# Hash attention and an MLP on one core: the scale row and its product moved to the front, hash products ahead of the fillers, the last unit's sums cut in halves

## The chip, the cores and the metric

The kernel runs on one core of a Trainium2 chip. A core has TensorE (PE; its weight loads are listed as PEld), VectorE (DVE), ScalarE (ACT), GpSimd (POOL) and SyncE (SP), which here only issues DMAs. Each engine executes its own instructions in the order in which they were written and waits on semaphores for the others. Matrix products land in PSUM, everything else lies in SBUF, inputs and outputs in the chip's memory (HBM). The metric is the device time of one execution in microseconds (us); the median of several runs is given. The profile is one further execution, recorded by the hardware profiler.

## The reference

Two layers. First, attention with a hash mask: q and k get six sign bits each from a random projection, and a query sees only the keys with the same six bits.

```python
q_bits = (np.einsum('bhsd,dk->bhsk', q, proj) > 0)
k_bits = (np.einsum('bhsd,dk->bhsk', k, proj) > 0)
mask = q_bucket[:, :, :, None] == k_bucket[:, :, None, :]
scores = np.where(mask, scale * np.matmul(q, k.transpose(0, 1, 3, 2)), -1000000000.0)
attn = softmax(scores)                       # + 1e-09 in the denominator
x = np.matmul(attn, v)                       # -> (B, S, H * D)
xn = (x - mu) / np.sqrt(var + 1e-06) * g_ln  # over the last axis
out = x + np.maximum(xn @ w_ch1, 0.0) @ w_ch2
```

The shapes: 4 batches, 8 heads, 768 positions, 64 numbers per head; the MLP goes from 512 to 2048 and back. All inputs and the output are f32.

## The kernel before

**Units.** The work is cut in 12 units `u`: batch `u // 3`, and 256 of the 768 queries, all eight heads. Within a unit there are two groups `g` of four heads and three pieces `kp` of 256 keys; `s` from 0 to 71 counts unit, group and piece.

**The order is written out by hand.** `ORDER` is one long string of words such as `S.t.0.2`: a function's name, the engine (t TensorE, v VectorE, a ScalarE, p GpSimd, s SyncE) and its arguments. The program walks through it and issues each word's instructions to its engine. What counts on the chip is only the order of the words of one engine among themselves, and who waits for whose data or buffer. `SLOTS` gives, for each kind of tile, which of its few buffers the next new tile takes; a tile waits until the last user of the buffer's former tile is done. PSUM has three large buffers (`pp`: scores `sc`, sums `acc`, and the tile of the fillers) and two small ones (`f`: everything else).

**The words that the change and the prediction touch**, with the line of their instruction in the profile:

- `lx`, `lv` (L373, L465) load q, k and v of batch 0; `LX`, `lv` (L508, L467) those of the later batches; `lw1`, `lw2` (L446, L457, from GpSimd) the weights; `lg` (L433) the row `moe_g_ln`. `gx` (L505) is a one-column memset through which a load waits for its buffer.
- `warm` (L363) eight products of ones with ones; `wm` (L366) one more such product each. They compute nothing that is used and are called fillers.
- `tn` (L304) turns a piece of q (t = 0) or k (t = 1) of batch 0, two transposes each; `ca` (L311 to L315) casts the turned piece to bf16; `ha` (L394) is the hash product of a piece, `bh` (L307) makes its bits; `hc`, `bc`, `sl`, `bi` (L405, L307, L418, L428/L430) do the same in another layout for the later q pieces. For batches 1 to 3 it is `tu` (L304, eight pieces), `CA`, `hm` (L526) and `bt` (L307), and the bits go through HBM (`mw`, `mr`, L544 and L547).
- `S` (L570) scores of one `s`: the bits as extra rows of the product, then q by k. `E` (L576) the exponential of two heads. `A` (L595) attention weights by v, summed in `acc`. `cv` (L473, L475) casts v; `sq` (L494) or `su`/`sp` sum v over the keys, `sc` (L500, L502) copies that sum, for rows in which the mask leaves nothing.
- `na`, `nb` (L608 to L617) normalise, `nc`, `ag`, `ce`, `rs` (L621 to L636) are the layer norm.
- `gt` (L437) turns the row `moe_g_ln` into a column, with eight small products, `gc` (L443) copies it to `gT`. In unit 0 the normalised x is transposed on TensorE (`ft`, L644) and scaled with gT on the way out (`fc`, L652); later units go through a DMA transpose (`fl`, L639), and `wg` (L452, L454) scales the weights with gT once.
- `F` (L659) an eighth of the first MLP product, `R` (L667, L669) its relu. In unit 0 the second product is plain (`D`, `Z`). From unit 1 on it is done by seven products of half-size blocks instead of eight: `P` (L725) the products 1 to 7, `ss` (L710) the four sums of blocks of the hidden layer that they need, `sw` (L699) those of the weights, once, and `Y` (L730) adds products to the output. `O` (L742, L744) stores.

The sums that `ss` makes, for `k` = 1 to 4, each over eight blocks of 128 hidden numbers by 128 queries:

```python
1: (1, Hq(u, 1, 0), Hq(u, 1, 1), AOP.add),
2: (2, None, Hq(u, 0, 0), AOP.subtract),          # None: sum 1
3: (3, Hq(u, 0, 0), Hq(u, 1, 0), AOP.subtract),
4: (4, Hq(u, 0, 1), None, AOP.subtract),          # None: sum 2
```

Block `n` of the halves comes from products `F` 0, 1 (blocks 0 to 3), 2, 3 (4 to 7), 4, 5 (8 to 11) and 6, 7 (12 to 15).

## Time and profile before

| what | us |
|---|---|
| median of three runs | 295.71 (293.08 to 297.33) |
| the profiled execution | 294.86 |
| its span in the trace | 293.2 |
| TensorE busy | 285.6 (97% of the span) |
| VectorE busy | 206.8 (71%) |
| ScalarE busy | 206.2 (70%) |
| GpSimd busy | 54.0 (18%) |

A row of the instructions in order of time reads: start, duration, engine, line, operation, what it writes and reads, the shapes, how many, and in brackets the idle time of the engine ahead of it and who ended that. A row with several instructions runs from the start of the first to the end of the last. A matmul's recorded duration is longer than its step, since products overlap in the array; the distance of starts is the step. A row of the busy time by stage gives the stretch, its length, and the busy time (and count) of TensorE, weight loads, VectorE, ScalarE and GpSimd in it, then the clock granted to TensorE, the share of the DMA engines and GB/s. The chain of work that ended last is followed back from the last instruction.

### The profile page before, as it was taken

What the parts mean: (1) busy time and instruction counts of PE and PEld (TensorE: products, weight loads), DVE (VectorE), ACT (ScalarE), POOL (GpSimd) and SP (SyncE); (2) the same over time, 40 slices, a digit from 0 to 9 for tenths busy, and PEclk for the clock granted to TensorE, in tenths of its full rate; (3) what the DMA queues carried; (4) which work ended last, traced back from release to release, by engine and by line L of the source; (5) the groups of instructions that cost most, each with busy time, mean ns of one, the idle gap of its engine ahead of it and who ended that gap; (6) DMA issues with size and microseconds to landing.
All of it is one profiled execution on the core that took longest, in us unless ns stands there. A gap on an engine that the chain in (4) does not pass through costs nothing.

```text
span 293.2 us, 10524 instructions
## 1 busy us (share of the span) xinstructions
PE 285.6 (97%) x4650; PEld 227.7 (78%) x4650; DVE 206.8 (71%) x474; ACT 206.2 (70%) x236; POOL 54.0 (18%) x88
## 2 busy tenths in 40 slices
PE   8999999999999999999999999999999999999994
PEld 4677778648788887878778778877888878897883
DVE  4757899996769795797667995866666654773433
ACT  4689999998966978784865896887793694515240
POOL 5261325222423005000300107210010010000000
PEclk9999999999999999999999999999999999999999
DMA  6999997747744692362330352230410402304022
GB/s 223 302 319 250 216 277 133 139 134 171 174 122 131 134 307 76 127 189 51 98 82 1 83 132 63 60 61 3 92 37 2 74 2 52 78 6 104 2 72 73
DMA packets 31055, 34.10 MB, mean 116 GB/s; under 512 B 15521, under 2 KB 27809, under 8 KB 31010
## 3 DMA queue, kind: packets, MB, share of 16 engines
q1 hardware_dynamic: 25938, 28.72, 35.6%
q0 software_dynamic: 4224, 4.19, 8.9%
q8 instruction: 36, 0.59, 0.9%
q10 hardware_dynamic: 848, 0.53, 0.7%
q14 instruction: 9, 0.07, 0.1%
HBM read 27.86 MB, written 6.88 MB: 118 GB/s over the span
## 4 chain that ended last, share of the span: by engine, by line
PE 91%; DMA 3%; DVE 2%; SPq 1%; ACT 1%; issue 0%; ACTq 0%; DVEq 0%
PE f L659 27%; PE sc L570 18%; PE X L725 13%; PE acc L595 12%; PE Yb L725 7%; PE hp L526 3%; PE Ya L725 3%; PE hf L394 3%; PE f L674 2%; PE warm L363 1%; ACT E L576 1%; DMA G<-Bd 1%; DMA Bd<-B 1%; PE warm L366 1%; DMA xnT<-xc 1%; SPq L547 1%
## 5 line engine op out<-in xcount | busy, mean ns | idle before, releaser
L576 ACT ACTIVATE E<-sc,bias_sb 128x1024 bf16<-128x1024 f32 x144 | 153.1, 1111 | 36.0 <-PE sc L570 32.6
L659 PE MATMUL f<-xnT,w_sb 128*128 128x256 bf16 x768 | 94.2, 273 | 0.7 <-DMA xnT<-xc 0.6
L659 PEld LDWEIGHTS <-w_sb 128*128 128x128 bf16 x768 | 71.4, 98 | 13.6 <-issue 5.7
L667 ACT ACTIVATE hb<-f 128x512 bf16<-128x512 f32 x67 | 39.6, 598 | 34.5 <-PE f L659 34.5
L570 PE MATMUL sc<-qb,kb 32*128 32x256 bf16 x1152 | 52.5, 267 | 0.0
L595 PEld LDWEIGHTS <-E 128*128 128x128 bf16 x1152 | 40.8, 98 | 4.0 <-issue 2.5
L595 PE MATMUL acc<-vaug,E 128*128 128x65 bf16 x1152 | 43.7, 194 | 0.1
L570 PE MATMUL sc<-G 6*128 6x256 bf16 (+1 forms) x576 | 42.7, 273 | 1.1 <-ACT E L576 0.8
L725 PEld LDWEIGHTS <-hb 128*128 128x128 bf16 x352 | 33.4, 98 | 5.4 <-issue 1.3
L570 PEld LDWEIGHTS <-kb 32*128 32x128 bf16 x1152 | 30.5, 93 | 1.5
L635 POOL TENSOR_SCALAR rs<-mv 128x2 f32<-128x2 f32 x12 | 3.3, 277 | 150.4 <-DVE mv L624 150.4
L730 DVE TENSOR_TENSOR x<-X,x 128x256 f32<-128x256 f32 x44 | 18.4, 419 | 16.5 <-PE X L725 16.3
L570 PEld LDWEIGHTS <-G 6*128 6x128 bf16 (+1 forms) x576 | 16.0, 91 | 16.7 <-issue 13.3
L725 PEld LDWEIGHTS <-S 128*128 128x128 bf16 x264 | 25.0, 98 | 4.8 <-issue 1.4
L669 DVE TENSOR_SCALAR hb<-f 128x512 bf16<-128x512 f32 x29 | 19.7, 681 | 12.0 <-PE f L659 11.8
L304 DVE STREAM_TRANSPOSE T<-X 128x384 f32<-128x384 f32 (+2 forms) x52 | 26.1, 535 | 0.0
L725 PE MATMUL Yb<-w_sb,S 128*128 128x256 bf16 x176 | 22.9, 273 | 0.0
L608 DVE SCALAR_TENSOR_TENSOR y<-vsB,acc 128x520 f32<-128x520 f32 x24 | 16.5, 689 | 8.1 <-PE acc L595 7.8
L725 PE MATMUL X<-wt,hb 128*128 128x256 bf16 x168 | 21.8, 273 | 0.0
L617 DVE TENSOR_TENSOR x<-y,rc 128x512 f32<-128x512 f32 x24 | 17.8, 742 | 0.8
L621 DVE BATCH_NORM_STATS2 st<-x 128x6 f32<-128x256 f32 x48 | 17.4, 412 | 0.2
L730 DVE TENSOR_TENSOR x<-Yb,x 128x256 f32<-128x256 f32 x22 | 9.2, 420 | 9.5 <-PE Yb L725 9.5
(95 smaller groups left out, 268.3 us busy)
## 6 DMA issues: line engine op xcount, KB each, us to landing
out_dram<-x SPq DMA_DIRECT2D x45, 128.0 KB
X<-in_k_dram SPq DMA_DIRECT2D x7, 768.0 KB
vn<-in_v_dram SPq DMA_DIRECT2D x24, 192.0 KB
X<-in_q_dram SPq DMA_DIRECT2D x6, 768.0 KB
w_sb<-in_moe_w_ch_dram POOLq DMA_DIRECT2D x8, 512.0 KB, 10.8
vn<-in_v_dram SPq DMA_DIRECT2D x2, 768.0 KB
X<-in_q_dram SPq DMA_DIRECT2D x2, 512.0 KB
Bd<-B SPq DMA_DIRECT2D x6, 96.0 KB
```

What stands on the lines that cost most here:

```text
L304: nc.vector.transpose(d[:, j], s[:, j, kj0 : kj0 + n])
L570: nc.tensor.matmul(sc(s, i // 2)[:, i % 2, 256 * kk : 256 * kk + 256], lh, rh, start=(rep == 0), stop=(rep == 2), skip_group_check=True,)
L576: nc.scalar.activation(E(s)[:, heads(h)], sc(s, h), AF.Exp, scale=EXP_SCALE, bias=bias_sb)
L595: nc.tensor.matmul(acc[:, qt, (D + 1) * i : (D + 1) * (i + 1)], E(s)[:, i, 256 * kk + P * qt : 256 * kk + P * qt + P], vaug(u // 3)[:, 4 * ...
L608: nc.vector.scalar_tensor_tensor(yt(u, g), vs, EPS_ROW, made[f"acc{u}{g}"][:, :, :A], op0=AOP.mult, op1=AOP.add,)
L617: nc.vector.tensor_tensor(xo, a[:, :, :, 0:D], rc.to_broadcast([P, 2, 4, D]), op=AOP.mult)
L621: nc.vector.bn_stats(stats(u)[:, qt, g], xt(u)[:, qt, 256 * g : 256 * g + 256])
L659: nc.tensor.matmul(f1[:, n].rearrange("p (t x) -> p t x", t=2), w1_sb[:, dt, P * nt : P * nt + P], xnT(u)[:, :, dt], start=(dt == 0), stop ...
L667: nc.scalar.activation(hb(u)[:, 2 * p : 2 * p + 2], f1, AF.Relu)
L669: eng.tensor_scalar_max(hb(u)[:, 2 * p : 2 * p + 2], f1, 0.0)
L725: nc.tensor.matmul(f2, lh[:, n], rh[:, n], start=(first and n == 0), stop=(n == 7), skip_group_check=True)
L730: nc.vector.tensor_tensor(x, made[f"{prod(u, k)}{u}"], x, op=AOP.add)
```

## The change

Four things change; the computation and the number of products stay the same.

1. `lg` becomes the second load on SyncE's queue, and `gt` and `gc` move from the end of unit 0's attention (behind `S` 6) to a place ahead of `S` 1.
2. The first two hash products (`ha` 0.0.0, 0.1.0) come directly behind `warm`; four of the eight `wm` stood ahead of them. The eight `wm` now stand singly or in small groups between later hash products and scores.
3. The order of the front stage, up to about `S` 16, is another one on every engine. Some work changes its engine: two casts of unit 0's second head group go to VectorE (`ca` 1.1.1 from GpSimd, `ca` 1.0.0 from ScalarE), the copy `sc` 0.0 goes from VectorE to ScalarE, and two v casts swap GpSimd and ScalarE. `wg` 3 and the loads of batch 1's second group come earlier. The buffers in `SLOTS` (E, X, f, pp, tp) are given out anew to match. Past `S` 16 TensorE's order is the same up to unit 11; the words of SyncE are written at other places of the string, in the same order among themselves.
4. `ss` takes an optional part, four of the eight blocks. In unit 11 the four sums are made in halves: first halves behind `R` 11.1, second halves where the whole sums stood. The products `F` of unit 11 change from 4 0 2 5 7 1 6 3 to 4 0 5 1 7 2 6 3, so that the first halves' blocks come first.

The diff, cut to the front, the tail, the buffers and the function:

```diff
 ORDER = """
-lp.a lx.a.0.1.0.1 lx.s.0.0.0.1 lx.s.0.1.1.3 lx.s.1.1.0.3 lx.s.1.0.0.1 lv.s.0.0.4 lx.s.0.0.1.3 lv.s.0.4.4 lx.s.1.0.1.3
-lg.s on.p.0 mem.v tab.a pf.v warm.t wm.t.0 wm.t.1 wm.t.2 wm.t.3
-sel.p tn.v.0.0.0 p32.p tn.v.0.1.0 on.p.1 lw1.p.3 ca.a.0.0.0 pmem.p ha.t.0.1.0 bh.v.0.1.0
-ha.t.0.0.0 ca.a.0.1.0 bh.v.0.0.0 wm.t.7 wm.t.5 wm.t.4 tn.v.0.1.1 ca.p.0.1.1 tn.v.0.1.2 S.t.0.2
-E.a.0.0 E.a.0.1 ha.t.0.1.1 bh.v.0.1.1 ha.t.0.1.2 bh.v.0.1.2 wm.t.6 tn.v.1.1.1 ca.p.1.1.1 ca.a.0.1.2
-tn.v.1.1.0 S.t.1.2 E.a.1.1 tn.v.1.0.0 ha.t.1.1.1 bh.v.1.1.1 cv.p.0.0.0 tn.v.1.1.2 gx.p.1.0.0 S.t.2.2
-cv.p.0.0.2 cv.p.0.4.2 ca.p.1.1.2 E.a.1.0 ca.a.1.0.0 lv.s.1.0.3 lw1.p.1 ha.t.1.0.0 bh.v.1.0.0 gx.p.1.0.1
-LX.s.1.0.0 ha.t.1.1.2 bh.v.1.1.2 E.a.2.1 lw1.p.0 ca.v.1.1.0 LX.s.1.0.1 tn.v.0.0.1 S.t.4.2 E.a.2.0
-lv.s.1.0.2 ca.v.0.0.1 E.a.4.1 ha.t.1.1.0 A.t.0.2 A.t.2.2 sq.t.0.0 E.a.4.0 bh.v.1.1.0 S.t.3.2
-sc.v.0.0 A.t.1.2 cv.a.0.4.0 E.a.3.1 hc.t.0.0.1 E.a.3.0 lw2.p.0 na.v.0.0 S.t.5.2 bc.v.0.0.1
...
-ca.a.1.0.1 bi.a.1.0.1 S.t.6.2 gt.t E.a.6.0 nc.v.0.1 ag.v.0.1 S.t.7.2 ag.v.0.0 ce.v.0.1
-ft.t.0.1 ce.v.0.0 gc.v E.a.6.1 E.a.7.0 ft.t.0.0 S.t.9.2 E.a.7.1 E.a.9.0 fc.v.0.1
...
-E.a.11.0 rs.p.0 tu.v.1.0.0.2 R.v.0.0 E.a.11.1 CA.v.1.0.0 S.t.14.2 E.a.14.0 nb.v.1.0 bc.v.1.0.2
-E.a.14.1 hm.t.1.0 ca.v.1.0.2 lv.s.1.0.0 S.t.12.2 wg.v.3 sl.t.1.0.2 bi.a.1.0.2 bt.v.1.0 mw.s.1.0
...
+lp.a lx.a.0.1.0.1 lx.s.0.0.0.1 lg.s lx.s.0.1.1.3 lx.s.1.1.0.3 lx.s.1.0.0.1 lv.s.0.0.4 lx.s.0.0.1.3 lv.s.0.4.4
+lx.s.1.0.1.3 on.p.0 mem.v tab.a pf.v warm.t sel.p tn.v.0.0.0 p32.p on.p.1
+lw1.p.3 ha.t.0.0.0 tn.v.0.1.0 ca.a.0.0.0 ha.t.0.1.0 bh.v.0.0.0 bh.v.0.1.0 wm.t.6 ca.a.0.1.0 tn.v.0.1.2
+ca.a.0.1.2 wm.t.3 wm.t.5 tn.v.0.1.1 ca.p.0.1.1 S.t.0.2 E.a.0.1 E.a.0.0 ha.t.0.1.2 bh.v.0.1.2
+cv.p.0.0.2 ha.t.0.1.1 wm.t.7 bh.v.0.1.1 wm.t.2 pmem.p gt.t gc.v S.t.1.2 E.a.1.0
+gx.p.1.0.0 LX.s.1.0.0 E.a.1.1 wm.t.0 tn.v.1.1.1 ca.v.1.1.1 tn.v.1.0.0 ca.v.1.0.0 wm.t.1 ha.t.1.1.1
+bh.v.1.1.1 wm.t.4 S.t.2.2 cv.p.0.0.0 ha.t.1.0.0 tn.v.1.1.0 ha.t.1.1.0 bh.v.1.0.0 E.a.2.1 tn.v.1.1.2
+ca.p.1.1.2 S.t.4.2 E.a.2.0 lv.s.1.0.2 A.t.2.2 sq.t.0.0 bh.v.1.1.0 A.t.0.2 E.a.4.0 ca.v.1.1.0
+cv.p.0.4.0 tn.v.0.0.1 ca.v.0.0.1 E.a.4.1 A.t.1.2 sc.a.0.0 cv.a.0.4.2 na.v.0.0 S.t.3.2 E.a.3.0
+tn.v.0.0.2 lw1.p.1 ha.t.1.1.2 bh.v.1.1.2 tn.v.1.0.1 E.a.3.1 hc.t.0.0.1 S.t.5.2 E.a.5.1 E.a.5.0
...
+hc.t.0.0.2 E.a.6.0 S.t.7.2 E.a.6.1 ce.v.0.0 ce.v.0.1 ft.t.0.0 lw2.p.0 E.a.7.0 fc.v.0.0
+E.a.7.1 S.t.9.2 E.a.9.0 ft.t.0.1 E.a.9.1 A.t.7.2 LX.s.1.1.0 bc.v.0.0.2 ca.a.0.0.2 A.t.6.2
+fc.v.0.1 sl.t.0.0.2 F.t.0.7 tu.v.1.0.0.1 R.a.0.7 lv.s.1.0.1 lv.s.1.0.3 tu.v.1.0.0.2 tu.v.1.0.0.0 lw2.p.3
+S.t.10.2 E.a.10.0 bi.v.0.0.2 E.a.10.1 F.t.0.6 F.t.0.3 gx.p.1.1.1 tn.v.1.0.2 R.a.0.3 R.a.0.6
+wg.v.3 LX.s.1.1.1 tu.v.1.0.1.0 A.t.8.2 S.t.11.2 na.v.1.0 E.a.11.1 ca.v.1.0.2 tu.v.1.0.1.3 E.a.11.0
+F.t.0.0 R.v.0.0 tu.v.1.0.1.1 hc.t.1.0.2 bc.v.1.0.2 S.t.14.2 E.a.14.0 E.a.14.1 tu.v.1.0.1.2 lw2.p.1
+hm.t.1.0 bt.v.1.0 mw.s.1.0 S.t.12.2 sl.t.1.0.2 A.t.10.2 bi.a.1.0.2 CA.p.1.0.1 A.t.9.2 A.t.11.2
...
-R.a.11.0 Y.v.10.7 P.t.10.4 Y.v.10.4 O.s.10.2 F.t.11.2 R.a.11.2 F.t.11.5 R.a.11.5 F.t.11.7
-F.t.11.1 R.a.11.7 R.a.11.1 F.t.11.6 F.t.11.3 R.a.11.6 P.t.11.2 R.a.11.3 ss.v.11.1 P.t.11.1
-Y.v.11.2 ss.v.11.2 Y.v.11.1 ss.v.11.4 P.t.11.5 P.t.11.6 O.s.10.0 Y.v.11.5 P.t.11.3 ss.v.11.3
-Y.v.11.6 P.t.11.7 O.s.10.1 Y.v.11.3 Y.v.11.7 O.s.10.3 O.a.11.0.1 O.s.11.0.0 Y.v.11.7.1.0 O.s.11.1.0.1
-O.a.11.1.1.1 P.t.11.4 Y.v.11.4 O.a.11.1.1.0 O.s.11.1.0.0
+R.a.11.0 Y.v.10.7 P.t.10.4 Y.v.10.4 O.s.10.2 O.s.10.0 O.s.10.1 O.s.10.3 F.t.11.5 R.a.11.5
+F.t.11.1 R.a.11.1 ss.v.11.1.0 ss.v.11.2.0 ss.v.11.3.0 ss.v.11.4.0 F.t.11.7 F.t.11.2 R.a.11.7 R.a.11.2
+F.t.11.6 F.t.11.3 R.a.11.6 R.a.11.3 P.t.11.2 ss.v.11.1.1 P.t.11.1 Y.v.11.2 P.t.11.5 ss.v.11.2.1
+Y.v.11.1 P.t.11.6 ss.v.11.4.1 Y.v.11.5 P.t.11.3 ss.v.11.3.1 Y.v.11.6 P.t.11.7 Y.v.11.3 O.a.11.0.1
+O.s.11.0.0 Y.v.11.7 O.s.11.1.0.1 O.a.11.1.1.1 Y.v.11.7.1.0 P.t.11.4 Y.v.11.4 O.a.11.1.1.0 O.s.11.1.0.0
 """
...
-    pp="0121020102011202102102102121021020212012012012112012010121021202012010201202101202102010202120212110201101002120102102101210021202120102100210210102010201012102102120210",
+    pp="0122120102102101201201201212021021202102102102002102101020120212102101210212010212012101212021202001210010112021012012010201120212021012011201201012101210102012012021201",
...
-    def ss(eng, u, k):
+    def ss(eng, u, k, *part):
+        r = slice(4 * part[0], 4 * part[0] + 4) if part else slice(0, 8)
...
-        eng.tensor_tensor(Ss(u, out), in0, in1, op=op)
+        eng.tensor_tensor(Ss(u, out)[:, r], in0[:, r], in1[:, r], op=op)
```

At the head of the `pp` string one sees the two buffers of `S` 1: before `S` 0 took buffers 1 and 2 and `S` 1 took 1 and 0 (0 was the fillers'); after, `S` 1 takes 2 and 1, and the fillers keep 0 until `S` 2.

More of the change, by code (lines that the diff above doesn't have):

```diff
@@ new lines @@
+S.t.36.2 P.t.3.2 R.a.3.2 E.a.36.1 nb.v.5.1 su.p.2.4 ss.v.3.1 Y.v.3.2 P.t.3.1 E.a.36.0
+S.t.39.2 E.a.39.1 E.a.39.0 ce.v.4.0 fl.s.4.0 Y.v.3.1 nc.v.5.0 A.t.37.2 P.t.3.5 ss.v.3.2
+ss.v.3.4 A.t.36.2 Y.v.3.5 cv.v.2.4.0 P.t.3.6 Y.v.3.6 P.t.3.3 A.t.38.2 ss.v.3.3 S.t.40.2
+Y.v.3.3 E.a.40.0 E.a.40.1 P.t.3.7 nc.v.5.1 Y.v.3.7 tu.v.3.0.0.1 F.t.4.3 ag.v.5.0 R.v.4.3
+P.t.3.4 Y.v.3.4 O.s.3.1 O.s.3.0 O.s.3.3 S.t.41.2 E.a.41.1 E.a.41.0 sp.t.2.0 sc.v.2.0
+F.t.4.0 ag.v.5.1 rs.p.5 F.t.4.4 R.a.4.4 na.v.6.0 R.v.4.0 ce.v.5.1 fl.s.5.1 S.t.44.2
@@ L154 @@
     st="010101010101",
-    tp="012102101201210210210210210120210210210120120",
+    tp="012012012012102102102102102012102102102012012",
     vaug="0101",
```

161 lines of the change are left out of this document (76 added, 85 removed).

## The prediction

> **What bounds the kernel now.** I read the page first, then the busy time by stage, then the instructions in order of time at both ends. From the page, the busy shares and the chain of work that ended last:
>
> ```profile
> PE 285.6 (97%) x4650; PEld 227.7 (78%) x4650; DVE 206.8 (71%) x474; ACT 206.2 (70%) x236; POOL 54.0 (18%) x88
> PE 91%; DMA 3%; DVE 2%; SPq 1%; ACT 1%; issue 0%; ACTq 0%; DVEq 0%
> ```
>
> TensorE (PE) is the bound, by share and by chain. The same by stage (PE, weight loads, VectorE, ScalarE, GpSimd, then clock, DMA share, GB/s):
>
> ```profile
> 9.78:21.09 11.31, 11.31 (x165) 8.32 (x166) 7.54 (x21) 10.52 (x12) 5.85 (x8) 1.00 1.09 332
> 21.09:34.43 13.34, 12.13 (x277) 9.74 (x274) 10.86 (x29) 13.16 (x15) 3.25 (x7) 1.00 1.03 216
> 34.43:48.40 13.97, 13.90 (x317) 10.64 (x315) 12.44 (x27) 13.06 (x16) 6.14 (x8) 1.00 1.09 257
> 48.40:267.39 218.99, 218.69 (x3670) 176.74 (x3670) 160.44 (x354) 160.27 (x182) 34.52 (x48) 1.00 0.37 93
> ```
>
> From 48.4 to 267.4 us PE is busy 218.69 of 218.99 us. The PE words and their order are the same there in both versions, and SyncE (SP), which there keeps its order of words too, only has its words written in other places between those of other engines; a queue does not see that. So this stage can only be moved as a whole. What the change can win or lose lies before 48.4 us and after 277 us. In the two stages from 9.8 to 34.4 us ScalarE (ACT) is the full one: 10.52 of 11.31 and 13.16 of 13.34 us, against 13.06 of 13.97 later, when PE is full as well.
>
> **The change part by part: the last unit.** From the instructions in order of time, the end of before:
>
> ```profile
> 283.08 0.69 DVE L710 TENSOR_TENSOR S<-hb 128x1024 bf16<-128x1024 bf16 x1 [5.44 <-ACT hb L667]
> 283.13 1.04 PE L725 MATMUL X<-w_sb,hb 128*128 128x256 bf16 x8
> 284.03 0.68 DVE L710 TENSOR_TENSOR S<-S,hb 128x1024 bf16<-128x1024 bf16 x1
> 284.63 0.42 DVE L730 TENSOR_TENSOR x<-X,x 128x256 f32<-128x256 f32 x1
> 284.96 0.68 DVE L710 TENSOR_TENSOR S<-hb,S 128x1024 bf16<-128x1024 bf16 x1
> 285.10 1.03 PE L725 MATMUL X<-wt,S 128*128 128x256 bf16 x8
> 287.83 1.04 PE L725 MATMUL Yc<-wt,hb 128*128 128x256 bf16 x8
> 28.21 0.69 DVE L617 TENSOR_TENSOR x<-y,rc 128x512 f32<-128x512 f32 x1
> ```
>
> and from the chain, products with nothing in the way:
>
> ```profile
> 262.42 4.38 PE f L659 x40
> ```
>
> Products 1, 5, 6, 3, 7 and 4 of the last unit start from 283.13 to 287.83: five steps in 4.70 us. VectorE paces them: a sum S starts at 284.03 and the next at 284.96, 0.93 us for a sum and an output addition, and product 6 starts at 285.10, just after the addition that must read X (284.63 + 0.42 = 285.05). With nothing in the way forty matmuls, five such products, take 4.38 us by the chain, 0.87 or 0.88 each. So the most that this part can win is about **0.35 us**.
>
> A half sum is not in the trace. An addition of 512 f32 per partition takes 0.69 (L617), of 256 takes 0.42 (L730): half the size saves 0.27. For a sum of 0.68 that makes 0.41; the bounds are 0.34 (half) and 0.68 (nothing saved). At 0.41 the pace of VectorE falls from 0.93 to about 0.66, under the 0.87 of PE, and the whole 0.35 is won; at 0.68 nothing is. I take 0.41, since the same engine and kind of operation shows it. The four first halves (4 x 0.41 = 1.6 us) run while VectorE has nothing else to do (5.44 us idle ahead of 283.08); to make them possible products F 5 and 1 come before 7 and 2, four products of the same length in another order, at no cost while PE goes on without a gap. [...]
>
> **The front, up to the first scores.** The first instructions that count, in order of time:
>
> ```profile
> 1.11 3.60 PE L363 MATMUL warm<-ones 128*128 128x512 bf16 x8 [1.11 <-DVE bias_sb L320]
> 4.34 1.66 DVE L304 STREAM_TRANSPOSE tp<-X 128x256 f32<-128x256 f32 x4 [1.21 <-DMA X<-in_q_dram]
> 4.50 1.91 PE L366 MATMUL warm<-ones 128*128 128x512 bf16 x4
> 6.21 2.12 PE L394 MATMUL hf<-tp,pfull 128*128 128x256 f32 x8
> 7.50 0.42 DVE L307 TENSOR_SCALAR G<-hf 128x256 bf16<-128x256 f32 x1 [1.51 <-PE hf L394]
> 8.16 0.81 PE L366 MATMUL warm<-ones 128*128 128x512 bf16 x3
> 8.91 0.29 PE L570 MATMUL sc<-G 32*128 32x256 bf16 x4
> 9.78 2.12 ACT L576 ACTIVATE E<-sc,bias_sb 128x1024 bf16<-128x1024 f32 x2 [2.66 <-PE sc L570]
> 11.79 1.11 ACT L311 ACTIVATE kb<-tp 128x512 bf16<-128x512 f32 x1
> 12.80 2.12 ACT L576 ACTIVATE E<-sc,bias_sb 128x1024 bf16<-128x1024 f32 x2
> 14.81 0.63 ACT L311 ACTIVATE qb<-tp 128x512 bf16<-128x512 f32 x1
> ```
>
> The clock column says 1.00 throughout, but the filler product takes 3.60/8 = 0.45 us up to 4.7 us and 0.81/3 = 0.27 at 8.2: the first six microseconds run at about half rate. Before, two hash products wait behind four fillers and start at 6.21. In the new order the first starts when q is turned, half of the first turning row, 4.34 + 0.83 = 5.2. Until about 6.4 it goes at half rate, which costs 0.6 us more than the 2.12 us of the row, so both end near 7.9 (before: 8.33), the bits near 8.3, and the first scores start at 8.3 instead of **8.91**: 0.6 us won. The fillers stay eight in number, three of them here inside that wait.
>
> Then ScalarE. The cast of the third k piece (1.11 us) comes ahead of the first exponentials; it needs a turning that VectorE does after the bits (8.3 + 0.8 = 9.1), so cast to 10.2, exponentials of scores 0 to 12.3, where before exponentials and cast ended at 12.9: 0.6 won. This is given back: scores 1 get the two PSUM buffers of scores 0, because the fillers keep the third to the end, where before one half had the fillers' buffer. They wait for the last exponential of 0: 12.3 to 13.1, exponentials of 1 from 13.1 against 12.80. Scores 2 stand on PE behind a hash product whose turning stands on VectorE behind the copy of gT, and that behind the eight small products of Scale's row. These take:
>
> ```profile
> 28.02 0.72 PE L437 MATMUL gp<-one,grow 1*128 1x1 f32 x6
> 29.45 0.28 PE L570 MATMUL sc<-G 32*128 32x256 bf16 x2 [0.36 <-ACT E L576]
> 30.77 0.15 DVE L443 COPY gT<-gp 128x4 f32<-128x4 f32 x1
> 31.03 1.29 DVE L652 TENSOR_TENSOR xnT<-ft,gT 128x512 bf16<-128x512 bf16 x2
> ```
>
> Six of eight take 0.72, so all about 0.9; in the new place they fall in the wait of scores 1 for the exponentials (11.4 to 12.3), which hides them; if that wait were gone they would cost their 0.9 us. Their row is now SP's second load and not its ninth; the load ahead of it had landed by 4.34 (turning row), so I take it as there by 11. VectorE goes on at 12.5: turning to 13.2, hash product to 14.3, scores 2 from 14.6 to 15.4, exponentials from 15.5; before, 15.33. ScalarE has lost one cast of 0.63 (14.81) in between, and spends it waiting.
>
> ```profile
> 16.66 0.29 PE L570 MATMUL sc<-G 32*128 32x256 bf16 x4
> 17.10 0.64 DVE L315 CAST kb<-tp 128x512 bf16<-128x512 f32 x1
> 18.45 0.43 DVE L313 TENSOR_SCALAR qb<-tp 128x512 bf16<-128x512 f32 x1
> 19.55 0.83 ACT L473 CAST vaug<-vn 128x768 bf16<-128x768 f32 x1
> 20.24 0.42 DVE L502 COPY vsB<-vp 128x256 f32<-128x256 f32 x1 [1.02 <-PE vp L494]
> 21.09 6.32 ACT L576 ACTIVATE E<-sc,bias_sb 128x1024 bf16<-128x1024 f32 x6 [0.70 <-PE sc L570]
> ```
>
> VectorE takes over two casts, of prices 0.64 and 0.43 by these rows, ahead of the bits that scores 4 need; two hash products stand ahead of scores 4 where three were spread before. I get 17.1 for scores 4 (16.66 before), exponentials 17.9 to 20.0, then the copy of vsB, moved here from VectorE (0.4), and the v cast (0.83): 21.2 for exponentials 3, against **21.09**. Before, ScalarE stood idle 0.70 us there, waiting for PE; that wait goes, and the moved copy and the later scores fill it. The bound on the good side: the work that ScalarE has from the first cast on (1.0 + 8 x 1.0 + 0.4 + 0.8 = 10.2 us, an exponential at 6.32/6 or a little less) after 9.1, without any wait, ends at 19.3, 1.8 us early.
>
> **The front, 21 to 48 us.** Up to the last exponential of the stage both orders give ScalarE the same fourteen instructions, and it is full (13.16 of 13.34), so a tie stays a tie. What the early gT takes off here, 0.9 us of PE and 0.15 of VectorE ahead of the scaled transposes (31.03), lies beside exponentials that scores 7 wait for anyway (29.45); what can be won is the idle rest of ScalarE, 0.2 us. Then, from the time list and the chain:
>
> ```profile
> 38.62 1.03 DVE L304 STREAM_TRANSPOSE T<-X 128x384 f32<-128x384 f32 x2
> 40.77 1.51 PE L526 MATMUL hp<-T,p 128*32 128x192 f32 x32
> 42.53 1.14 DVE L454 TENSOR_SCALAR w_sb<-w_sb,gT 128x512 bf16<-128x512 bf16 x4
> 48.40 0.29 PE L570 MATMUL sc<-G 32*128 32x256 bf16 x4
> ```
>
> The hash of the next batch (40.77) needs eight turned pieces; before, the last was ready at 39.65. Now the weight scaling (1.14) and a q cast come ahead of the last pieces, and a relu that waits for product F 0 (end 39.1 by my count) stands in front of two of them: 39.3 + 0.7 + 0.5 + 0.2 + 0.5 gives 41.2, so the hash comes 0.4 us later. Behind it VectorE has the scaling's 1.14 us less to do, which gives back between nothing and the 0.4; I take 0.3, since by its row the scaling stood right in that stretch. **Sum of the front:** +0.1 - 0.2 + 0.4 - 0.3 = 0, scores 16 at 48.4 again, with bounds of -1.8 (above) and +1.5 (first rival).
>
> **The sum.** -0.35 and 0 on the profiled execution of 294.86 us (span 293.2 and 1.7 around it) make 294.5. That execution lies 0.85 under the median of the three runs, 295.71 (293.08 to 297.33); on that footing I forecast **295.3 us**, no change that can be told: 2%, 5.9 us, is about what a measurement of this kernel can tell.
>
> **Rivals.**
> 1. *The clock rises later (slower).* PE goes from product to product from 1.11 to 8.9 before, and the rate doubles near 6.4 (four fillers, 4.50 to 6.41, are all slow), 5.3 us after the start. In the new order the fillers end at 4.5 and PE idles to 5.2. If this break starts the count again, the rate doubles at 10.5: two hash products at half rate cost 2.12 us more, 0.6 of it already counted: +1.5; three fillers (0.2 each) and the first scores (0.8) make it 2.9. The first scores then end near 12, the first exponentials start 2.0 to 2.2 us after the 10.2 of the sum, and ScalarE's later waits at scores 2 and 4 (0.3 each) take up 0.6 of that: +1.5 us at exponentials 3. ScalarE is full from there, so nothing gives it back: 296.8. It decides from the point at which the break is long enough to count. Against it: a break of 0.7 in 5.3 us is short. [...] 0.12.
> 2. *VectorE becomes the bound near 41 us (slower).* The relu in front of the turned pieces waits one product longer (0.87 us) than I count, which makes the hash late by 0.4 + 0.8 = 1.2 us, and VectorE, 12.44 busy of 13.97 us there, does not catch up: 295.3 + 1.2 = 296.5. For it: the two moved casts and the scaling all come earlier on it. Against it: the same instructions in sum. 0.15.
> 3. *The front gives its full gain (faster).* The waits that I set on ScalarE at scores 1, 2 and 4 (0.8, 0.3, 0.3) close, if PE and VectorE steps are shorter than I add them, up to the bound of 1.8: 295.7 - 1.8 - 0.35 gives 293.5. 0.20.
> 4. *The halves do nothing,* because the output additions pace the products by themselves: 0.35 less, 295.7. 0.05.
>
> **Chances and range.** The forecast (its own range 294.3 to 296.3) has 0.48. From 293.5 and 296.8, and about 1.2 to 1.6 us on each side for the scatter that the three runs show (their ends are 2.6 below and 1.6 above the median), the range is 292.3 to 298.3. No rival reaches 2% by itself: faster by over 2% needs 5.9 us, while PE stands idle for 13.34 - 12.13 = 1.2 us in the stage from 21 to 34 us and for less elsewhere, 0.02; slower by over 2% needs a stall that I have not found, 0.04; within, 0.94.
>
> **What would show it.** First scores near 8.3; a pause of PE between 4.5 and 5.2 and filler products of 0.22 us a step after it (rival 1: still 0.43 after 7); exponentials 1 close to 13.1 with ScalarE idle before them; exponentials 3 at 21.2; hash of the next batch near 41; scores 16 at 48.4; at the end seven products at steps of 0.87 and half sums of 0.41. The forecast is wrong if scores 16 start over 1 us from 48.4, or if the stage after that shows new gaps on PE.

## The result, and the profile after

The changed kernel is slightly slower: median 295.88 us of 20 executions (294.22 to 299.37), before 294.10 of 20 (292.48 to 297.33), ratio **1.0045, 95% interval 1.0023 to 1.0066**. A second set gave 295.65 against 294.46, ratio 1.0033 (1.0008 to 1.0058). The forecast, 295.3 or 0.35 us less than before, lies on the other side of that interval. That 295.88 falls into the forecast's own range, 294.3 to 296.3, is luck: the range stands on the median of three executions, 295.71, and over twenty the kernel before has 294.10, 1.6 us less. Executions more than 1.5% above the fastest of the same kernel, here two of the changed one at 298.92 and 299.37 us, are left out of the ratios. The profiled execution took 296.68 us (span 294.9), 1.8 us more than that of before.

From the page after, busy shares and the chain that ended last:

```profile
PE 285.6 (97%) x4650; PEld 228.5 (77%) x4650; DVE 208.2 (71%) x479; ACT 206.4 (70%) x236; POOL 53.2 (18%) x87
PE 92%; DMA 4%; SPq 1%; ACT 1%; DVE 1%; issue 0%
```

TensorE has as many products and as much busy time as before, and the kernel still hangs on it. By stage (columns as before: PE, weight loads, VectorE, ScalarE, GpSimd, then clock, DMA share, GB/s), cut at exponentials 3 and scores 16:

```profile
9.78:21.19 11.41, 11.41 (x180) 8.49 (x179) 9.06 (x22) 9.45 (x11) 4.46 (x8) 1.00 1.10 343
21.19:34.43 13.24, 11.31 (x261) 8.42 (x261) 9.68 (x27) 12.67 (x15) 3.90 (x8) 0.91 1.04 255
34.43:50.29 15.86, 15.53 (x313) 12.17 (x311) 11.88 (x27) 13.79 (x17) 3.77 (x4) 0.96 0.96 202
50.29:269.70 219.41, 218.14 (x3667) 176.61 (x3667) 160.60 (x355) 159.83 (x182) 37.07 (x51) 1.00 0.36 92
```

Exponentials 3 start at 21.19 (before 21.09), scores 16 at 50.29 (before 48.40): the front loses 1.9 us, nearly all in the two middle rows, and there the granted clock is 0.91 and 0.96. In steps of two microseconds, after, then before (only the last two):

```profile
28.00:30.00 2.00, 1.32 (x50) 0.81 (x42) 1.90 (x5) 1.69 (x4) 0.00 (x0) 1.00 1.11 363
30.00:32.00 2.00, 1.43 (x36) 0.86 (x32) 1.91 (x6) 2.00 (x3) 0.00 (x0) 1.00 1.08 350
32.00:34.00 2.00, 2.00 (x37) 1.56 (x30) 0.60 (x3) 1.89 (x3) 0.00 (x0) 0.53 1.11 267
34.00:36.00 2.00, 2.00 (x34) 1.91 (x32) 2.00 (x6) 1.54 (x3) 0.10 (x1) 0.61 1.20 238
```

```profile
32.00:34.00 2.00, 1.92 (x37) 1.61 (x29) 2.00 (x6) 2.00 (x3) 0.95 (x3) 1.00 0.83 139
34.00:36.00 2.00, 2.00 (x53) 1.42 (x52) 1.52 (x5) 1.77 (x4) 1.41 (x4) 1.00 0.88 261
```

TensorE idles 1.25 us of the four from 28 to 32, and then **the granted clock falls to half**, for 3.41 us by the clock record (32.13 to 35.55). In the chain of after, 32 products of `A` take 1.76 us there (33.60), where 32 of them at full clock take 0.98 (44.91):

```profile
33.60 1.76 PE acc L595 x32
...
44.91 0.98 PE acc L595 x32
```

Near 130 us one more wait is longer than before (1.27 against 0.30 us, for the hash bits that come back from HBM); scores 39 are 2.66 us late, of which 0.30 is got back by 270 us, 0.34 in the last seven products and 0.23 behind them.

### The profile page after: what moved, and what is told of

Same layout as the page of the kernel before. It is cut to its first block, busy times and chain, and to the rows that moved or that the text cites. A ratio compares the mean times of both kernels' runs of the same rounds, so it can differ in the third digit from the quotient of the medians.

```text
span 294.9 us, 10531 instructions
## 1 busy us (share of the span) xinstructions
PE 285.6 (97%) x4650; PEld 228.5 (77%) x4650; DVE 208.2 (71%) x479; ACT 206.4 (70%) x236; POOL 53.2 (18%) x87
## 4 chain that ended last, share of the span: by engine, by line
PE 92%; DMA 4%; SPq 1%; ACT 1%; DVE 1%; issue 0%
PE f L659 28%; PE sc L570 19%; PE acc L595 13%; PE X L726 13%; PE Yb L726 7%; PE hp L526 3%; PE Ya L726 3%; PE f L674 2%; PE hf L394 2%; DMA X<-in_k_dram 2%; DMA G<-Bd 1%; DMA xnT<-xc 1%; ACT E L576 1%; PE vp L494 0%; SPq L547 0%
## 5 line engine op out<-in xcount | busy, mean ns | idle before, releaser
L659 PEld LDWEIGHTS <-w_sb 128*128 128x128 bf16 x768 | 71.4, 98 | 13.1 <-issue 5.4
L595 PEld LDWEIGHTS <-E 128*128 128x128 bf16 x1152 | 41.7, 99 | 4.0 <-issue 3.0
L595 PE MATMUL acc<-vaug,E 128*128 128x65 bf16 x1152 | 44.5, 196 | 0.3 <-issue 0.3
L617 DVE TENSOR_TENSOR x<-y,rc 128x512 f32<-128x512 f32 x24 | 16.6, 692 | 0.8
```

The lines of the kernel that those rows point to most:

```text
L595: nc.tensor.matmul(acc[:, qt, (D + 1) * i : (D + 1) * (i + 1)], E(s)[:, i, 256 * kk + P * qt : 256 * kk + P * qt + P], vaug(u // 3)[:, 4 * ...
L617: nc.vector.tensor_tensor(xo, a[:, :, :, 0:D], rc.to_broadcast([P, 2, 4, D]), op=AOP.mult)
L659: nc.tensor.matmul(f1[:, n].rearrange("p (t x) -> p t x", t=2), w1_sb[:, dt, P * nt : P * nt + P], xnT(u)[:, :, dt], start=(dt == 0), stop ...
```

## The experiments

"Ratio" is to the kernel before, timed beside it, with its 95% interval. One half-clock stretch makes a mean granted clock of 0.994 (half of 3.41 us is 0.6% of the time in which the clock is recorded), so executions are also counted in which it was 0.994 or less.

### The two ends apart

`e_tail` is before with the last unit of after, `e_front` the changed kernel with the last unit of before.

> The kernel before with the change's last unit alone (sums in halves, products F in the order 4 0 5 1 7 2 6 3); the front is that of before. If the halves win what was forecast, the seven last products go at steps of 0.87 instead of 0.93 us and the median falls by 0.35 us against before (ratio 0.9988). If the loss of the changed kernel sits in its last unit, this kernel is slower than before by about 1.3 us (ratio 1.0045). If the halves do nothing: ratio 1.000.

> The changed kernel with the last unit of before: whole sums, products F in the old order. If the loss is in the front and the tail wins 0.35 us, this one is 1.3 + 0.35 = 1.65 us slower than before (ratio 1.0056). In some executions the clock granted to TensorE should fall to half for 3.4 us between 28 and 36 us (mean clock 0.994). If the tail makes the loss: ratio 1.000.

Measured: `e_tail` 294.69 us, ratio 0.9994 (0.9970 to 1.0017); `e_front` 296.55, ratio 1.0056 (1.0024 to 1.0089). The last unit in the chain of before, and in that of after (first and last of its seven products):

```profile
282.42 0.87 PE Ya L725 x8
...
288.00 0.89 PE Yc L725 x8
```

```profile
284.78 0.87 PE Ya L726 x8
...
290.02 0.89 PE Yc L726 x8
```

From 5.58 to 5.24 us: the tail wins 0.34 us, and `e_tail` shows the same 5.24. The loss is in the front.

### The half clock near 30 us

`e_fill` adds 17 filler products where TensorE waits anyway; `e_thin` the same 17, one column wide; `e_gtback` puts the small products of Scale's row back; `after_again` is the changed kernel once more.

```diff
 e_fill   (wf: ones by ones, 192 columns into unread columns 64:256 of the tile of hc 0.0.2)
-hc.t.0.0.2 ... S.t.7.2 ... ft.t.0.0 ... S.t.9.2 ... ft.t.0.1
+hc.t.0.0.2 ... wf x7 S.t.7.2 ... wf x3 ft.t.0.0 ... wf x4 S.t.9.2 ... wf x3 ft.t.0.1
 e_thin   the same, wf with one column
 e_gtback
-pmem.p gt.t gc.v S.t.1.2 ... S.t.7.2 ... ce.v.0.0
+pmem.p S.t.1.2 ... gt.t S.t.7.2 ... gc.v ce.v.0.0
```

> The changed kernel with 17 additional filler products of 192 columns (ones by ones, into columns of a PSUM tile that nothing reads) between scores 6 and the second scaled transpose, in places where TensorE waits anyway: seven ahead of scores 7, three ahead of the first transpose, four ahead of scores 9, three ahead of the second transpose. Clock theory: no execution shows the half clock between 28 and 36 us, scores 10 start near 35.0, the time falls by 0.5 to 1.5 us against the changed kernel's 295.9. Rival, the chain of transposes and scaled copies through one PSUM buffer, or the late hash of batch 1: the fillers change nothing, scores 10 still start over 1 us later than before's 34.70 and the time stays 295.9 or rises by the 0.1 to 0.3 us of the fillers.

> The kernel with the 17 fillers at the same places, each one column wide instead of 192. If what keeps the clock is that products are issued (busy time in the profile), the executions keep full clock as with the wide fillers: none with a mean clock at or under 0.994, median 294.5. If it is the work that the array does, one column does next to nothing: a quarter of the executions show a mean clock at or under 0.994 as in the changed kernel, median near 295.9.

> The changed kernel with the eight small products of Scale's row (gt) and their copy (gc) back behind scores 6, as before; the load of the row stays early. Clock theory: these 0.9 us of TensorE fill the stretch from 28.7 to 32.1 us in which it stands idle for 1.2 us in the changed kernel, the clock stays at 1.0, scores 10 start near 35.0 instead of 36.4, and the time falls by 0.5 to 1.5 us against the changed kernel. Rival, the late hash of batch 1 (turned pieces behind the weight scaling and a relu on VectorE): nothing of that is touched, scores 16 stay about 1.5 us late and the time is that of the changed kernel, 295.9, within 0.4 us.

> The changed kernel once more, for a second profiled execution and twelve more times. If the half clock between 32.1 and 35.6 us depends on where the clock's windows of 3.41 us lie in an execution, which the moment of the first full clock shows (4.83 us in the first profile), a third of the executions have a mean clock near 0.994 and those are 1.5 us longer than the others; a profile with another moment of the first full clock need not have it, and its scores 16 then start near 49 instead of 50.3. If the half clock belongs to the order itself, every profile has it.

Measured: `e_fill` 294.47 us, ratio 1.0014 (0.9989 to 1.0039); `e_thin` 294.81, 1.0022 (0.9997 to 1.0046); `e_gtback` 296.03, 1.0060 (1.0027 to 1.0093). Busy time from 30 to 32 us in `e_fill`, `e_thin` and `after_again`:

```profile
30.00:32.00 2.00, 2.00 (x37) 1.34 (x35) 1.87 (x8) 2.00 (x3) 0.00 (x0) 1.00 1.08 301
```

```profile
30.00:32.00 2.00, 1.66 (x39) 1.16 (x39) 1.91 (x7) 2.00 (x3) 0.00 (x0) 1.00 1.05 296
```

```profile
30.00:32.00 2.00, 1.01 (x26) 0.66 (x24) 1.97 (x7) 2.00 (x3) 0.00 (x0) 1.00 1.10 350
```

The second profile of the changed kernel idles even longer there and keeps its clock; its first full clock came at 6.36 us instead of 4.83. In every trace the record changes only at multiples of 3.41 us after the first full clock (in the first profile of the changed kernel after 8, 9 and 85 of them, in that of before after 84), so where the idle stretch lies in such a window differs from execution to execution. (The least busy 3.41 us near 30 us are 63% busy in both profiles; in the first they are just one window, in the second they lie across two.) The counts: mean clock of 0.994 or less in 9 of 32 executions of the changed kernel, 2 of 12 of `e_front`, 3 of 12 of `e_gtback` and 4 of 12 of `e_thin`, 18 of 68 in all; in none of 58 of the kernels with its front and the wide fillers (`e_fill` and, below, `e_vec`, `e_cast`, `e_nowm`, `e_lean`). Before has 12 of 138. So the half clock belongs to the front in about a quarter of the executions (that it lies near 30 us is seen in one trace), wide fillers end it, and **what counts here is how wide the products are, not that one is issued**: with one-column products at the same places 4 of 12 executions have 0.994 or less, and with Scale's row (one column each) put back 3 of 12, so that moving it is not the cause.

The times bear this out less sharply than the counts. In the first twenty, five with 0.994 lie at 296.4 to 296.7 us and the median of those above 0.994 at 295.4; in the second set the two with 0.994 lie at 294.3 and 296.3, around their median of 295.65. The interval of `e_fill` overlaps with both of the changed kernel. And the wide fillers are not free: from scores 8 to scores 10 it is 11.93 us in the first profile with its half clock, 10.39 in `after_again` and `e_front`, which keep their clock without fillers, and 10.72 in `e_fill`. So a half clock costs 1.5 us in a quarter of the executions, about 0.4 on average by these numbers, and the 17 fillers cost 0.3 in each.

### The parts of the change on the order of before

All four have the new last unit. `e_fillb` adds ten wide fillers ahead of scores 7 and the first scaled transpose; `e_hash` takes only the early hash products and leaves four old fillers out; `e_best` is both; `e_gtfront` takes only Scale's row to the front.

```diff
 e_hash
-warm.t wm.t.0 wm.t.1 wm.t.2 wm.t.3 ... ha.t.0.1.0 bh.v.0.1.0 ha.t.0.0.0 ... bh.v.0.0.0 wm.t.7 wm.t.5 wm.t.4
+warm.t ... ha.t.0.0.0 ... ha.t.0.1.0 ... bh.v.0.0.0 bh.v.0.1.0 wm.t.0 wm.t.1 wm.t.2
 e_gtfront
-lg.s on.p.0 ... S.t.1.2 ... S.t.6.2 gt.t ... gc.v
+lx.s.0.0.0.1 lg.s ... gt.t gc.v S.t.1.2 ... S.t.6.2
```

> The kernel before with the change's last unit, and ten filler products of 192 columns (into unread columns of the tile of Scale's row, which is made 512 wide for it): seven ahead of scores 7, three ahead of the first scaled transpose; the front is otherwise that of before. If before too loses its clock there in some executions (its TensorE is busy for 0.79 of a 3.4 us stretch near 29 us, 0.63 in the changed kernel), the slow executions go and the median falls by up to 0.3 us against the kernel with the tail alone: ratio to before 0.998. If the clock holds in before without help: ratio 0.9994, as with the tail alone. If the fillers cost time of their own: ratio 1.000 to 1.001.

> The kernel before with the change's last unit and only the first part of the front: the two first hash products directly behind the eight products of the first word, three fillers behind them, the four other fillers that stood there left out (they compute nothing); everything else in the order of before. If the early hash products are worth the 0.6 us that the forecast gave them and nothing behind takes them back, first scores start at 8.3, scores 16 near 47.8 and the ratio to before is 0.9975 (the tail's 0.35 us with it). Rival: TensorE is the full engine from 9.8 to 21 us in this order, but the pieces are turned one after the other on VectorE, so the first scores come early and scores 2 and 4 at their old times: scores 16 at 48.3, ratio 0.9990. Second rival: the pause of TensorE at 4.5 us delays the full clock by a window of 3.4 us in some executions: ratio 1.001 or more, scattered.

> The early hash products, the change's last unit and the ten fillers of the last two kernels together, on the order of before. If the effects add: scores 16 near 47.8, no execution with the half clock near 30 us, ratio to before 0.996 to 0.9975, faster than both kernels. If the front gives nothing: 0.9985 to 0.9995.

> The early hash products, the halved sums and the ten wide fillers on the order of before, again, with more times: if the six times of the first run (292.45 to 292.94) are typical, ratio to before 0.992 to 0.996. If they were lucky: 0.997, the ratio of the kernel without the early hash products.

> The other way round: the kernel before with the change's last unit and only the first part of the change, the load of Scale's row second on the queue and its eight products and their copy ahead of scores 1; nothing else of the front. If TensorE's chain is what counts there, scores 1 and the exponentials behind them come 0.5 to 0.9 us later than in before, scores 16 at 48.9 to 49.3, ratio to before 1.0005 to 1.002 (with the tail's gain in it). If they are hidden: scores 16 at 48.4, ratio 0.9994. If the place that they leave, behind scores 6, lets the clock fall more often: more executions with a mean clock at or under 0.994 than the one in ten of before.

Measured: `e_fillb` 293.74 us, ratio 0.9975 (0.9951 to 0.9998); `e_hash` 294.11, 0.9979 (0.9949 to 1.0010); `e_best` 292.56 of six, 0.9924 (0.9896 to 0.9952), again 293.34 of twelve, 0.9972 (0.9946 to 0.9998); `e_gtfront` 295.40, 1.0022 (0.9991 to 1.0052). `e_best` is faster than both kernels, but by the second expectation the first six times were lucky: twelve more give the ratio of `e_fillb`, which does without the early hash products. ScalarE in the first profile of `e_best`:

```profile
8.99 2.12 ACT L583 ACTIVATE E<-sc,bias_sb 128x1024 bf16<-128x1024 f32 x2 [1.99 <-PE sc L577]
11.00 1.10 ACT L311 ACTIVATE kb<-tp 128x512 bf16<-128x512 f32 x1
12.01 2.12 ACT L583 ACTIVATE E<-sc,bias_sb 128x1024 bf16<-128x1024 f32 x2
...
20.29 4.31 ACT L583 ACTIVATE E<-sc,bias_sb 128x1024 bf16<-128x1024 f32 x4 [0.70 <-PE sc L577]
```

Each row is 0.8 us earlier than its like in before (9.78, 11.79, 12.80, 21.09), scores 16 at 47.51: with the exponentials ahead of the third k cast, the early hash products win their 0.6 to 0.8 us in this trace. In the other two traces that have them on this order the loads take it back. In `e_best_2` VectorE waits for a q piece, and scores 16 start at 48.25, as in `e_fillb` (48.22):

```profile
13.83 0.77 DVE L304 STREAM_TRANSPOSE tp<-X 128x256 f32<-128x256 f32 x2 [1.89 <-DMA X<-in_q_dram]
```

In `e_hash` the same wait is 1.30 us, its v load landed late as well (the v cast at 21.31), scores 16 start at 49.70, and 3 of 12 executions have the half clock. So what the early hash products are worth in the median is not shown.

Of the kernels with wide fillers on the order of before (`e_fillb`, `e_best`, `e_best_2`) 1 of 30 executions has 0.994 or less. Scale's row in the front of before is no gain: in `e_gtfront` exponentials 1 start 4.69 us after scores 0 instead of 3.89, so that the small products are not hidden in that order, and 3 of 12 executions have the half clock.

### VectorE's order, and a cast that takes twice its time

In the changed kernel scores 8 wait for bits (`bi` 0.0.1), and one cast on VectorE is long:

```profile
17.58 1.08 POOL L315 CAST kb<-tp 128x512 bf16<-128x512 f32 x1
...
17.75 1.39 DVE L315 CAST kb<-tp 128x512 bf16<-128x512 f32 x1
...
24.50 0.40 PE L570 MATMUL sc<-G 32*128 32x256 bf16 x4 [0.52 <-DVE G L430]
```

VectorE's cast (0.64 in before) takes 1.39 us beside GpSimd's and ends 0.48 us after it (19.14 against 18.66). `e_vec` takes two turned pieces out from ahead of the bits, `e_cast` moves GpSimd's cast; both carry the 17 fillers.

```diff
 e_vec
-tn.v.0.0.2 ... bh.v.1.1.2 tn.v.1.0.1 ... bc.v.0.0.1 hc.t.1.0.1 sl.t.0.0.1 bi.v.0.0.1 bc.v.1.0.1 S.t.8.2 ... nc.v.0.0
+bh.v.1.1.2 ... bc.v.0.0.1 sl.t.0.0.1 bi.v.0.0.1 tn.v.1.0.1 S.t.8.2 hc.t.1.0.1 bc.v.1.0.1 ... tn.v.0.0.2 nc.v.0.0
 e_cast
-ca.p.1.1.2 S.t.4.2 ... cv.p.0.4.0
+S.t.4.2 ... cv.p.0.4.0 ca.p.1.1.2
```

> The kernel with the 17 fillers between scores 6 and the second transpose, and on VectorE the two turned q pieces (tn 0.0.2 and tn 1.0.1, 0.76 us each) no longer ahead of bc 0.0.1 but behind bi 0.0.1, which makes the bits that scores 8 wait for; on TensorE hash product hc 1.0.1 goes behind scores 8, as before. Theory that VectorE's order makes scores 8 late: they start near 24.3 instead of 25.0, TensorE's wait of 0.5 us for those bits goes, scores 16 start 0.5 us earlier than in the kernel with the fillers alone (48.8 instead of 49.3), and the time falls by 0.5 us against it (ratio to before near 0.9995). Rival, ScalarE is full there and the time is set by its earlier waits (scores 1, 2 and 4): scores 16 at 49.2 again, time as with the fillers alone, ratio 1.001.

> The kernel with the 17 fillers, and on GpSimd the cast of a k piece (ca 1.1.2) moved behind the v cast (cv 0.4.0), so that it no longer runs at the same time as VectorE's cast (ca 1.1.0). Theory: the two block each other, VectorE's cast takes 1.39 us in every trace where GpSimd's cast starts just ahead of it and 0.64 where not; with the swap it takes 0.64, the bits for scores 8 are ready up to 0.7 us earlier (24.3 instead of 25.0), and scores 16 start 0.3 to 0.5 us earlier than 49.3; time 0.3 to 0.5 us under the kernel with the fillers alone, ratio to before near 1.000. Rival, the cast is long for another reason (the place of its input, the form of the cast): it stays at 1.39 and nothing changes. Second rival: ScalarE is full up to the last exponentials of scores 3, so the earlier bits gain nothing: cast 0.64, scores 16 at 49.3.

Measured: `e_vec` 297.01 us, ratio 1.0070 (1.0042 to 1.0097); `e_cast` 294.58, 0.9999 (0.9981 to 1.0018), not to be told from `e_fill`. In `e_cast`:

```profile
18.06 0.61 DVE L316 CAST kb<-tp 128x512 bf16<-128x512 f32 x1
...
20.45 1.09 POOL L316 CAST kb<-tp 128x512 bf16<-128x512 f32 x1
...
20.71 0.70 DVE L616 SCALAR_TENSOR_TENSOR y<-vsB,acc 128x520 f32<-128x520 f32 x1 [0.90 <-ACT vsB L508]
...
24.82 0.40 PE L578 MATMUL sc<-G 32*128 32x256 bf16 x4 [0.52 <-DVE G L438]
```

Apart from GpSimd's, VectorE's cast takes 0.61 us, beside it 1.38 in `e_fill`; but VectorE now waits 0.90 us for the copy of vsB, which the change gave to ScalarE, and TensorE still waits 0.52 for the bits. The long cast was covered, and the outcome is that of the second rival of that expectation, though the wait is for ScalarE's copy. In `e_vec` scores 8 came 0.36 us earlier against exponentials 3, and the first scaled transpose waits 0.9 us for VectorE, which has the pieces put off ahead of it. The hash of batch 1's second group waits 1.1 us more, at 57.4 us; that need not be the order, since `e_lean_3` (below), with VectorE's order of the changed kernel there, waits 1.05 us at the same place. In both, two instructions of VectorE ahead of it are long beside sums on GpSimd (from 48.77 us 2.28 and 1.48 in `e_vec`, from 49.14 us 1.94 and 1.48 in `e_lean_3`; 0.69 and 0.95 in `e_fill`). My theory on VectorE's order gained nothing.

### The old fillers in TensorE's chain

`e_nowm` is `e_fill` without `wm` 7, 2, 0, 1 and 4; `e_lean` also has Scale's products back behind scores 6 and four of the new fillers fewer.

```diff
 e_nowm
-S.t.0.2 ... ha.t.0.1.1 wm.t.7 ... wm.t.2 ... S.t.1.2 ... wm.t.0 ... wm.t.1 ha.t.1.1.1 ... wm.t.4 S.t.2.2
+S.t.0.2 ... ha.t.0.1.1 ... S.t.1.2 ... ha.t.1.1.1 ... S.t.2.2
```

> The kernel with the 17 fillers near 30 us, but without five of the eight old fillers (wm 7, 2, 0, 1, 4), those that the changed order puts between the first scores and scores 4; they compute nothing. Theory: from 9.3 to 18 us TensorE goes from product to product without a gap in the changed kernel, and these five (0.2 to 0.3 us each, 1.2 in all) stand in its chain ahead of scores 1, 2 and 4, so without them scores 4 start up to 0.9 us earlier (16.7 instead of 17.6), scores 16 start 0.3 to 0.8 us earlier (48.5 to 49.0 instead of 49.3), and the time falls by as much, ratio to before 0.998 to 1.000. Rival, the forecast's view: they lie in waits for the exponentials and for VectorE and cost nothing; scores 4 at 17.4 to 17.6, ratio 1.0014. Second rival: without them the clock is not held and the half clock comes earlier; slower, with mean clocks under 0.995.

> As the last kernel, and the eight small products of Scale's row with their copy (gt, gc) back behind scores 6, as before (four of the wide fillers there left out for them). If the small products too stand in TensorE's chain ahead of scores 1 (0.9 us, and VectorE waits 0.98 us for their copy), scores 4 start another 0.3 to 0.5 us earlier (16.2 to 16.4), exponentials 3 near 20.8 and scores 16 near 48.2, as early as in before or earlier; ratio to before 0.996 to 0.999. Forecast's view (hidden in the wait of scores 1 for the exponentials): as the last kernel.

Measured: `e_nowm` 294.09 us, ratio **0.9969** (0.9946 to 0.9991), faster than before; `e_lean` 296.99, 1.0045 (1.0013 to 1.0078). The fillers between scores 1 and 2 and ScalarE's next row in the changed kernel, then ScalarE in `e_nowm`:

```profile
12.69 0.61 PE L366 MATMUL warm<-ones 128*128 128x512 bf16 x2
...
13.99 0.38 PE L366 MATMUL warm<-ones 128*128 128x512 bf16 x1
...
15.30 2.12 ACT L576 ACTIVATE E<-sc,bias_sb 128x1024 bf16<-128x1024 f32 x2 [0.48 <-PE sc L570]
```

```profile
13.40 4.17 ACT L583 ACTIVATE E<-sc,bias_sb 128x1024 bf16<-128x1024 f32 x4 [0.82 <-PE sc L577]
```

Without them the exponentials of scores 1 and 2 run on without the 0.48 us wait. From exponentials 1 to exponentials 2 it is 2.05 us instead of 2.60. The wait of 0.82 ahead of exponentials 1 stays, with Scale's products in the front (`e_nowm`) or not (`e_lean`, 0.83): the small products are hidden there, as forecast, and three fillers were not.

By exponentials 3 about 0.3 us of this is left: from exponentials 0 to exponentials 3 it is 10.94 us in `e_nowm` and 10.90 to 10.99 in the traces of `e_lean`, 11.28 to 11.50 in `e_fill`, `e_cast` and `e_thin`. The expected scores 16 at 48.5 to 49.0 did not come: 49.64 in `e_nowm`, after a stop of TensorE of 0.52 us near 45 us, and 49.23 in `e_lean`. So the ratio of `e_nowm` shows a gain, and the traces show where 0.3 us of it come from.

`e_lean` had two kinds of times, five from 294.1 to 295.7 us and seven from 296.9 to 298.4, none with a half clock. Two more profiles:

> The kernel without five old fillers and with the small products at their old place, once more for its profile: seven of its twelve times lay near 297.5 us and five near 294.7, all with mean clocks of 0.997 to 1.0, and its first profile was one of the short ones (span 292.4). If this one is long, it shows where: a first full clock later than 7.9 us (a window of 3.41 us more at half rate; the mean clock counts only from the first full clock on), or a DMA that lands later (third k piece, v, the bits of a later batch) with TensorE waiting 1 to 3 us for it. If it is short, it is the same as the first.

> The same as the last one, a third profile: first full clock after 7.9 us, or a late DMA, if it is one of the long executions.

They took 294.06 and 297.49 us. The first is like the first profile; in the second, exponentials 3 are as early (21.28 against 21.23), and then TensorE stops in the middle of a group of products:

```profile
27.21 0.84 PE L602 MATMUL acc<-vaug,E 128*128 128x65 bf16 x22
29.06 0.48 PE L602 MATMUL acc<-vaug,E 128*128 128x65 bf16 x10 [1.01 <-issue]
```

"issue" is a wait for nothing that the profile shows. The transfers of one instruction queue, 16 KB each (36 in the first profile of the changed kernel, 0.59 MB; I take them for TensorE's own instructions, which are 9300 of the 10531 there), started at 20.04 and 26.61 us in this execution and at 18.14 and 21.84 in the short one; a first stop (0.29 us) and this one end 2.73 and 2.45 us after these starts. With a third stop near 47 us (0.66) they make 1.96 of the 3.4 us between the two executions; 1.05 is the wait for turned pieces at 57.4 us. So the long kind is, by this one trace, in the main TensorE waiting for its instructions, which is inferred from these times; why the transfers start later stays open, and with it how much of the changed kernel's scatter is the same.

## Why the prediction was wrong

The step that failed is the sum of the front, "+0.1 - 0.2 + 0.4 - 0.3 = 0, scores 16 at 48.4 again". Scores 16 came at 50.29 in the profiled execution, and 0.6 to 1.5 us late in three profiles of the changed front that kept their clock (starts, us):

| | exponentials 0 | exponentials 3 | scores 10 | scores 16 |
|---|---|---|---|---|
| before | 9.78 | 21.09 | 34.70 | 48.40 |
| after, half clock | 9.77 | 21.19 | 36.43 | 50.29 |
| `after_again` | 10.62 | 22.35 | 35.83 | 49.86 |
| `e_front` | 10.32 | 21.61 | 35.45 | 49.27 |
| `e_gtback` | 9.92 | 21.22 | 35.09 | 49.04 |

- **The tail** was right in mechanism and size: 0.35 forecast (its two figures, 4.70 and 4.38, give 0.32), 0.34 in the trace, half sums of 0.42, products at 0.87.
- **Up to exponentials 3** most steps came out: scores 0 at 7.23 and 8.02 in the two profiles (8.3), exponentials 1 at 12.70 and 13.54 (13.1) with ScalarE idle 0.83 ahead of them (0.8), scores 4 at 17.11 and 17.96 (17.1), exponentials 3 at 21.19 and 22.35 (21.2). That the exponentials 0 now stand behind the cast of a k piece that lands at different times (they start from 9.77 to 10.62 us in the traces of the changed front) is a part of the scatter that I left out: exponentials 3 are 0.1 to 1.3 us later than before, not 0.1.
- **"The fillers stay eight in number, three of them here inside that wait"** is a step that failed: the other five I put nowhere. TensorE was full by the row that I quoted (11.31 of 11.31), and three of them cost 0.55 us between scores 1 and 2. From exponentials 0 to exponentials 3 the forecast has 11.0 us (10.2 to 21.2); the changed front took 11.3 to 11.7, and 10.9 to 11.0 without five of the fillers. By the times, taking the five out moves the ratio from 1.0014 and 0.9999 (`e_fill`, `e_cast`) to 0.9969; `e_lean`, which is without them too, is at 1.0045 with its long kind.
- **"A tie stays a tie"**, with 0.2 us to win from the idle rest of ScalarE between 21 and 34 us, is the other, and what it left out is the clock. From exponentials 3 to scores 10 before takes 13.61 us and the changed front at full clock 13.48 to 13.87, so that the tie nearly held, without the 0.2: scores 8 wait 0.52 us for bits (before 0.16, for an exponential), and 0.3 is won behind them. With the half clock it took 15.24. The waits for exponentials are as long as before (0.9 against 0.8 us in all), only with less of TensorE's work between them; that this goes with the half clock in a quarter of the executions is shown by the fillers (18 of 68 without wide ones, none of 58 with them), and the clock was not on my list for this stage. The 1.13 us by which scores 10 are late in `after_again` had been lost by exponentials 3 (1.26).
- **Rival 1** had the right resource and the wrong place. The pause at 4.5 us did nothing: TensorE's records go on from 4.52, and in the traces of the changed front the first full clock comes at 4.1 to 7.1 us, in those of before's order with the fillers first at 5.7 to 7.0. That a break starts the rise of the clock again was my estimate, and no run shows it. The half clock came at 32.13 us, behind a window of 3.41 us in which TensorE was busy for 63% of the time (2.16 of 3.41 us), with no wait longer than 0.68 us. The window, and the one behind it, in the changed kernel, then windows of `after_again`, `e_hash` and `e_front` behind which the clock stayed:

```profile
28.72:32.13 3.41, 2.16 (x58) 1.30 (x50) 3.25 (x10) 3.41 (x4) 0.00 (x0) 1.00 1.07 346
32.13:35.55 3.42, 3.42 (x59) 2.95 (x52) 2.02 (x5) 3.30 (x4) 0.00 (x0) 0.50 1.16 262
```

```profile
30.26:33.67 3.41, 2.34 (x53) 1.56 (x53) 2.76 (x9) 3.41 (x5) 0.00 (x0) 1.00 1.07 332
```

```profile
21.13:24.55 3.42, 1.92 (x56) 1.53 (x53) 1.08 (x3) 3.24 (x4) 3.21 (x5) 1.00 0.42 155
```

```profile
128.92:132.33 3.41, 1.91 (x47) 1.36 (x45) 2.84 (x7) 1.28 (x2) 0.00 (x0) 1.00 0.74 153
```

The last two were less busy (56%) than the one that cost the clock, so the busy share alone does not decide here. What else does, beyond the width of the products, stays open.

- **Rival 2**: the hash of the next batch came 1.64 and 1.04 us late, but no later than scores 10 ahead of it (1.73 and 1.13), so VectorE was not the bound there, and of the sum's +0.4 and -0.3 neither shows: behind scores 10 the hash is 0.1 us earlier than before (5.98 against 6.07 us). From scores 10 to scores 16 it is 13.70 us before and 13.8 to 14.0 in the changed front, with a stop of TensorE of 0.28 to 0.50 us near 45 us in each of its traces in the table. **Rivals 3 and 4** did not happen; the gain that rival 3 saw shows in one trace, of the early hash products on the order of before (`e_best`).

Set against each other: with the half clock and five fillers taken out, the new front (`e_nowm`, 0.9969) is by its time as good as the old one with fillers in the same stretch (`e_fillb`, 0.9975). So taking out the two costs that the forecast left out, the clock and the fillers, recovers the loss in the median of `e_nowm`; it does not in that of `e_lean`, whose long executions wait elsewhere. How much of the loss each is, the traces do not show: behind scores 16, where TensorE's order is the same, two of them with the same last unit still differ by 1.8 us (242.8 us to the end in `e_fill`, 244.6 in the first profile of the changed kernel).

## What to carry to other kernels

Where an engine is full in a stage, look for a place for every instruction that the change puts there, the ones that compute nothing too. Where TensorE waits in short gaps between narrow products (here for 1.25 us of 3.41), look at the granted clock, in several executions; with wide products into unread PSUM columns in these gaps none of 58 executions here had 0.994 or less, for 0.3 us of their own. Take a reordering apart, and time a part that looks good twice: `e_best` had a ratio of 0.992 in six executions and 0.997 in twelve more.
